# Loading k and q of the first batch whole, in place of by column ranges, in a linear-attention and MLP kernel

## The chip, the cores and the metric

The kernel runs on one core of a Trainium2 chip. The metric is device time in microseconds (us) of one execution; the median over several runs is compared. Engines: PE is the matmul array (PEld its weight loads), DVE the vector engine, ACT the activation engine, POOL the GpSimd engine, SP the engine that only issues transfers. Transfers issued from SP and from POOL run on the same 16 DMA engines, in two queues (q1 for SP, q0 for POOL).

## The reference

Inputs are q, k, v of shape (8, 8, 576, 64) (batch, heads, sequence, head size) and two MLP weights, 512x2048 and 2048x512. The attention is linear, with a cosine weighting of positions; its result, put back into rows of 512, goes through the MLP.

```
def phi(x, c, s):                       # c, s: cos and sin of pi/2 * position / S
    r = np.maximum(x, 0.0)
    return np.concatenate([r * c, r * s], axis=-1)
kv  = einsum('bhsf,bhsd->bhfd', phi(k), v)
z   = sum over s of phi(k)
num = einsum('bhsf,bhfd->bhsd', phi(q), kv)
den = einsum('bhsf,bhf->bhs', phi(q), z)[..., None] + 1e-06
x   = (num / den) as rows of 4608 x 512
h   = x @ w_in
out = (h * sigmoid(1.702 * h)) @ w_out
```

## The kernel before, in words

The eight batches go one after the other. For each, phi(k) and phi(q) are made on DVE and ACT, PE forms the 128x64 state of every head (kv), divides on DVE, transposes the result and runs the MLP; batch b+1's attention is woven into batch b's MLP. The order on every engine is written out by hand: instructions of an engine run in the order in which the program has them, with waits by semaphore.

The change touches the head of the program, the work on batch 0 ahead of its MLP. Names and lines there:

- L65 to L67: four loads from SP, k into kf and q into qf, 128 partitions by 4 head pairs by 576 floats. Each is cut by columns: k at 192, q at 256 floats. A column range of 64 floats is one position index j (0 to 8) of the nine that each partition holds, so k's first load has j = 0, 1, 2 and q's first j = 0 to 3. A partition's 576 floats of one head pair are contiguous in HBM, 2304 bytes.
- L153 and L154: a copy of one float of kf on POOL, in column 0. It keeps what follows it on POOL waiting until the load that holds that column has landed. Behind it POOL issues v of batch 0 in two loads (L156, into a part of the tile named sums, with a cast to bf16) and w_in's first two parts (L138).
- L161 trig: relu(k) times cos or sin for one j: two operations for each j, on DVE (L169), ACT (L167) or POOL. L819 to L827 give kr for j = 0, 1, 3, 4, 5 and the cos of 6 to DVE, j = 2, the sin of 6, and 7, 8 to ACT. L837 to L841 and L847 do the same for q into qn: j = 0, 1 on DVE, 2 to 5 and 7 on ACT, 6 and 8 on POOL.
- L778 idle: matmuls on zeros, 128x512, whose result nobody reads. L819 puts nine ahead of all else on PE. L831 puts two more between the k-sums.
- L247 ksum_mm: a matmul of kr for one j with a selector of 2 columns: the sum over k, over all nine j; L254 ksum_rows copies it out on DVE (L256), L258 ksum_turn turns it with small matmuls (L260) and a copy (L262).
- L197 qturn_pe: transposes of qn on PE (L205); L208 qevac copies them out on DVE (L215) or ACT (L213).
- L232 kv_mm: the products of kr and v, in two halves of four heads (L237), copied out by DVE (L245). L271 num_half, L286 div_half, L295 x_half: numerators (L276), division (L289, L291), transposes (L299) and a copy on ACT (L301). Then the first MLP matmuls (L882, L365).
- On POOL, behind the w_in loads: qn of j = 6, a copy of one element of v (L842, it waits for v's second load), the rest of w_in, k of batch 1, and parts of w_out.

Of the kernel before, what the change touches and what calls it, by code (L numbers as in the profile page):

```python
# [20 lines left out]
def kernel(  # L21
# [9 lines left out]
    nc = tc.nc  # L31
    B, H, S, D = q.shape
# [24 lines left out]
    def src_of(src, b, i0=0, i1=NI):  # L57
        return src[b, 2 * i0:2 * i1].rearrange("(i hh) (p j) d -> (hh p) i (j d)", hh=2, j=NS)

    qf = one.tile([128, 2560], F32, name="qf")  # L60
    kf, vf = [one.tile([128, NI, S], F32, name=n) for n in ("kf", "vf")]
    sums = one.tile([128, 4, d_ff], BF16, name="sums")
    vb = sums.rearrange("p n e -> p (n e)")[:, 0:NI * S].rearrange("p (i e) -> p i e", i=NI)
    qf0 = qf[:, 0:NI * S].rearrange("p (i e) -> p i e", i=NI)
    for t, src, cut in ((kf, k, 192), (qf0, q, 256)):  # L65
        nc.sync.dma_start(out=t[:, :, 0:cut], in_=src_of(src, 0)[:, :, 0:cut])
        nc.sync.dma_start(out=t[:, :, cut:S], in_=src_of(src, 0)[:, :, cut:S])  # L67


    NP = NS + 5  # L70
# [707 lines left out]
    def idle(n, cols=512):  # L778
        w = pmm.tile([128, 512], F32, name="mm")
        for _ in range(n):  # L780
            nc.tensor.matmul(w[:, 0:cols], warm[:, 0:128], warm[:, 0:cols], start=True, stop=True)
# [34 lines left out]
        xturn_evac(b, 4)  # L816


    idle(9)  # L819
    for j in (0, 1):  # L820
        trig(kr, kf, j)
    trig(kr, kf, 2, act=True)
# [321 lines left out]
```

## Time and profile before

| what | us |
|---|---|
| median of 3 runs (275.0 to 275.77) | 275.01 |
| the profiled execution's own time | 275.49 |
| its span in the profile | 273.4 |
| PE busy (97% of the span) | 265.7 |
| DVE busy (76%) | 207.8 |
| ACT busy (64%) | 174.8 |
| POOL busy (15%) | 42.4 |
| head, 0 to 15.3: PE busy / DVE busy / ACT busy | 12.70 / 10.29 / 12.15 |

Durations come from that one profiled execution, on a time scale that starts with its span. Busy time says how long an engine worked, not whether the end waited for it; for that the views of waits and of the chain that ended last are read. A duration in the timeline holds the pipeline's latency too, so consecutive operations overlap: what one costs its engine is the distance from its start to the next one's start. DMA rows give the time from the start of the issue to the landing that the waiting engine sees, and packets and bytes can be counted for any window of the span.

### The profile page before, as it was taken

To read this page: it belongs to the slowest core of one execution; us is meant where nothing else is said; L and a number is where in the kernel's file an instruction comes from. 1 tells how busy PE (TensorE), PEld (TensorE's weight loads), DVE (VectorE), ACT (ScalarE), POOL (GpSimd) and SP (SyncE) were. 2 spreads that over 40 slices of the span, in tenths; PEclk is the share of its full clock that TensorE was granted. 3 is DMA by queue.
4 is the path that set the end of the run, shared out by engine and by line. 5 is a ranking of instruction groups with operands and counts; after the bars stand their busy time and mean duration, and the time that the engine had idled before them with its cause. 6 is when DMAs were issued, how large, how long until landed. Compare 5 with 4: busy or idle time off the path is not lost.

```text
span 273.4 us, 7042 instructions
## 1 busy us (share of the span) xinstructions
PE 265.7 (97%) x2847; PEld 207.2 (76%) x2868; DVE 207.8 (76%) x487; ACT 174.8 (64%) x317; POOL 42.4 (15%) x71
## 2 busy tenths in 40 slices
PE   7899999999999999999999999999999999999994
PEld 2585645856987799778877887788778976999983
DVE  3956866698879798879887988888888994745741
ACT  5957642585199728983888387848783147677621
POOL 5691000000121012101110012001200173000410
PEclk9999999999999999999999999999999999999999
DMA  7999999999999996999898789796970654000333
GB/s 233 254 211 298 274 296 143 273 304 175 332 185 284 240 267 192 227 236 256 243 250 236 210 175 285 162 304 127 293 159 2 108 153 137 0 2 0 88 107 115
DMA packets 73663, 53.60 MB, mean 196 GB/s; under 512 B 52736, under 2 KB 63488, under 8 KB 73632
## 3 DMA queue, kind: packets, MB, share of 16 engines
q1 hardware_dynamic: 67504, 36.97, 58.3%
q0 software_dynamic: 6128, 16.19, 23.9%
q8 instruction: 22, 0.36, 0.6%
q14 instruction: 9, 0.07, 0.1%
HBM read 36.70 MB, written 9.44 MB: 169 GB/s over the span
## 4 chain that ended last, share of the span: by engine, by line
PE 93%; DMA 4%; DVE 1%; issue 1%; ACT 0%; POOL 0%
PE mm L520 31%; PE mm L658 16%; PE mm L365 13%; PE at L721 9%; PE mm L421 5%; PE at L520 4%; PE mm L396 4%; PE at L237 4%; PE at L310 3%; DMA sums<-in_v_dram 2%; DMA kf<-in_k_dram 1%; PE at L342 1%; PE mm L389 1%; DVE xn L325 1%; PE mm L205 0%
## 5 line engine op out<-in xcount | busy, mean ns | idle before, releaser
L520 PEld LDWEIGHTS <-sums 128*128 128x128 bf16 x448 | 42.5, 98 | 4.8
L526 POOL DMA_DIRECT2D out_dram<-ysb x24 | 17.4, 727 | 180.2 <-DVE inv L323 88.2
L520 PE MATMUL mm<-wsum,sums 128*128 128x256 bf16 x336 | 39.9, 272 | 0.0
L365 PE MATMUL mm<-xT,w_in 128*128 128x512 bf16 (+1 forms) x239 | 38.7, 305 | 0.5
L520 PEld LDWEIGHTS <-g 128*128 128x128 bf16 x336 | 32.0, 98 | 3.6
L371 ACT ACTIVATE g<-mm 128x512 bf16<-128x512 f32 x42 | 24.1, 598 | 10.9 <-PE mm L365 10.9
L365 PEld LDWEIGHTS <-w_in 128*128 128x128 bf16 x248 | 21.3, 114 | 11.5
L721 PE MATMUL at<-xT,w_in 128*128 128x512 bf16 x110 | 27.8, 379 | 0.5
L325 DVE TENSOR_TENSOR xn<-at,inv 128x512 bf16<-128x512 f32 x39 | 27.0, 691 | 1.3
L169 DVE TENSOR_SCALAR kr<-kf,cosw 128x256 bf16<-128x256 f32 x69 | 24.6, 357 | 3.0 <-DMA kf<-in_k_dram 3.0
L520 PE MATMUL mm<-w_out_sb,g 128*128 128x256 bf16 x224 | 26.6, 273 | 0.0
L169 DVE TENSOR_SCALAR kr<-kf,sinw 128x256 bf16<-128x256 f32 x68 | 23.6, 347 | 0.0
L658 PE MATMUL mm<-xT,w_in 128*128 128x256 bf16 x152 | 22.0, 273 | 0.0
L658 PE MATMUL mm<-xT,gt 128*128 128x256 bf16 x160 | 21.5, 272 | 0.0
L658 PEld LDWEIGHTS <-w_in 128*128 128x128 bf16 x168 | 18.6, 114 | 3.3
L183 ACT ACTIVATE qn<-qf,cosw 128x512 bf16<-128x512 f32 (+1 forms) x27 | 19.2, 711 | 1.5 <-DMA qf<-in_q_dram 1.1
L658 PEld LDWEIGHTS <-gt 128*128 128x128 bf16 x160 | 17.6, 113 | 3.0 <-issue 1.2
L721 PEld LDWEIGHTS <-w_in 128*128 128x128 bf16 x120 | 13.5, 113 | 8.2
L183 ACT ACTIVATE qn<-qf,sinw 128x512 bf16<-128x512 f32 (+1 forms) x27 | 19.2, 709 | 0.0
L371 ACT ACTIVATE g<-at 128x512 bf16<-128x512 f32 x30 | 17.5, 598 | 2.0 <-PE at L721 1.3
L535 ACT ACTIVATE kept_p<-mm 128x512 f32<-128x512 f32 (+1 forms) x15 | 8.5, 566 | 16.0 <-PE mm L520 16.0
L535 ACT ACTIVATE kept_u<-mm 128x512 f32<-128x512 f32 (+1 forms) x8 | 4.4, 544 | 20.6 <-PE mm L520 20.6
(175 smaller groups left out, 471.3 us busy)
## 6 DMA issues: line engine op xcount, KB each, us to landing
kf<-in_k_dram SPq DMA_DIRECT2D x6, 1152.0 KB, 9.2
vf<-in_v_dram SPq DMA_DIRECT2D x6, 1152.0 KB, 6.5
qf<-in_q_dram SPq DMA_DIRECT2D x6, 1024.0 KB, 6.3
out_dram<-ysb POOLq DMA_DIRECT2D x24, 256.0 KB, 5.1
w_out_sb<-in_moe_w_out_dram POOLq DMA_DIRECT2D x4, 512.0 KB, 17.7
kf<-in_k_dram POOLq DMA_DIRECT2D x1, 1152.0 KB, 13.4
vf<-in_v_dram POOLq DMA_DIRECT2D x1, 1152.0 KB, 20.8
w_in<-in_moe_w_in_dram POOLq DMA_DIRECT2D x2, 512.0 KB, 10.0
```

Of the source, the lines that this page charges most:

```text
L169: eng.tensor_scalar(o, i, 0.0, w[:, j:j + 1], op0=MAX, op1=MUL)
L183: nc.scalar.activation(o, i, AF.Relu, scale=sc)
L237: nc.tensor.matmul(st["kv", i][:, hh, ds(col, n)], kr[r, j, i, :], rhs(r, i, j), start=(j == 0), stop=(j == NS - 1))
L325: nc.vector.tensor_tensor(xn, pv[:, :, :, 0:64], inv.unsqueeze(3).to_broadcast([128, 2, 4, 64]), op=MUL)
L365: nc.tensor.matmul(hp[fc][:, t0:t1], wcol(kc, fc), x[b][:, kc, t0:t1], start=(kc == 0), stop=(kc == KC - 1))
L371: nc.scalar.activation(gT[fc // 4][:, fc % 4], hp.pop(fc), AF.Gelu_apprx_sigmoid)
L421: nc.tensor.matmul(yp[b, t, c0][:, c0:c1], w, w_out_sb[:, fc, c0:c1], start=(fc == 0), stop=(fc == FC - 1))
L520: nc.tensor.matmul(bank[to][c], lhs, rhs, start=opens, stop=(fc == HF - 1), skip_group_check=True)
L526: eng.dma_start(out=dst[:, 2 * i + c0:2 * i + c1, ts(n, HD)], in_=t[:, c0:c1])
L535: nc.scalar.activation(o, i, AF.Identity)
L658: nc.tensor.matmul(to[:, j], lhs, rhs, start=(opens and j == 0 and k == 0), stop=(k == 1), skip_group_check=True)
L721: nc.tensor.matmul(hp[fc], wcol(kc, fc), x[b][:, kc], start=(kc == 0), stop=(kc == KC - 1))
```

## The change

k and q of batch 0 are each loaded by one transfer of 128x4x576 floats, in pieces of 2304 bytes, where there were two. The order on SP is k, then q, as before. Every operation that waited for one of a tensor's two loads now waits for its only one. The nine idle matmuls at the start of PE's work become eleven. Nothing else changes in the order of any engine.

```
-    for t, src, cut in ((kf, k, 192), (qf0, q, 256)):
-        nc.sync.dma_start(out=t[:, :, 0:cut], in_=src_of(src, 0)[:, :, 0:cut])
-        nc.sync.dma_start(out=t[:, :, cut:S], in_=src_of(src, 0)[:, :, cut:S])
+    for t, src in ((kf, k), (qf0, q)):
+        nc.sync.dma_start(out=t, in_=src_of(src, 0))
...
-    idle(9)
+    idle(11)
```

## The prediction

> **What bounds the kernel now.** I read the page's busy shares first (PE 97% of the span), then who waited for whom on PE, because an edit to two loads can only cost what PE ends up waiting for. That view of the whole span has three rows:
>
> ```profile
> PE mm L781 <- DVE wsum L81: 1.2, 1, 1.2
> PE mm L251 <- DVE kr L169: 0.8, 2, 0.6
> PE mm L299 <- DVE xh L291: 0.2, 1, 0.2
> ```
>
> All three lie before 15.3 us: from there to the end PE waits for nobody for more than a few tenths in all. So the kernel is a head of some 15 us, paced by loads, DVE, ACT and small matmuls, and then a PE stream. A delay of the head moves the end by the same amount; a gain likewise. The change touches only the head.
>
> The chain that ended last, in order of time, names this in the head:
>
> ```profile
> 0.79 3.90 DMA kf<-in_k_dram
> 4.75 0.12 POOL gate L154
> 4.87 6.49 DMA sums<-in_v_dram
> ...
> 11.41 0.70 PE at L237 x36
> ```
>
> k's first column range lands, POOL's copy at L154 passes, v is issued, v lands, the k-v products start. But the timeline of DVE shows a second chain that is just as tight:
>
> ```profile
> 4.80 0.35 DVE L169 TENSOR_SCALAR kr<-kf,cosw 128x256 bf16<-128x256 f32 x1 [2.01 <-DMA kf<-in_k_dram]
> ...
> 5.33 0.56 DVE L169 TENSOR_SCALAR kr<-kf,cosw 128x256 bf16<-128x256 f32 x1
> 5.81 0.33 DVE L169 TENSOR_SCALAR kr<-kf,sinw 128x256 bf16<-128x256 f32 x1
> 6.84 0.59 DVE L169 TENSOR_SCALAR kr<-kf,cosw 128x256 bf16<-128x256 f32 x1 [0.70 <-DMA kf<-in_k_dram]
> ...
> 8.88 0.34 DVE L169 TENSOR_SCALAR kr<-kf,cosw 128x256 bf16<-128x256 f32 x1
> 9.14 0.34 DVE L169 TENSOR_SCALAR qn<-qf,cosw 128x256 bf16<-128x256 f32 x1
> ...
> 10.19 0.67 DVE L256 CAST wsum<-mm 2x512 bf16<-2x512 f32 x1
> 10.79 1.27 DVE L215 COPY qT<-mm 128x1024 bf16<-128x1024 bf16 x2
> 11.99 0.17 DVE L262 CAST kvs<-mm 128x8 bf16<-128x8 f32 x1
> 12.15 0.43 DVE L245 CAST kvs<-at 128x256 bf16<-128x256 f32 x1
> ```
>
> (Columns: start, duration, instruction, idle time before it.) DVE does 4 kr operations on the first column range, idles 0.70 us, and then has no gap from 6.84 to 12.58, up to the evacuation of the first k-v product. That product ended at 12.11 (11.41 and 0.70), and DVE was free for it at 12.15: v's chain and DVE's meet within 0.04 us.
>
> **The loads.** The rows of DMA issues (KB, us from issue to landing), each from a window of the trace: the two parts of k, and one later load of v, of the form that k's load now takes (576 contiguous floats, 512 pieces):
>
> ```profile
> kf<-in_k_dram SPq DMA_DIRECT2D x1, 384.0 KB, 3.9
> kf<-in_k_dram SPq DMA_DIRECT2D x1, 768.0 KB, 5.5
> vf<-in_v_dram SPq DMA_DIRECT2D x1, 1152.0 KB, 6.0
> ```
>
> Issued at 0.79 and 1.31, the parts land at 4.69 and about 6.8. Counted in quarter microseconds, the first packets move in the one from 1.75; by 3.0 some 165 KB have moved (1 KB = 1000 bytes in my byte counts), and then the rate is 332 GB/s with 768-byte packets and 399 with 1536-byte ones. k's 1180 KB are through at about 5.67; the landing comes 1.1 us later.
>
> What one transfer does to this, from two sides. First, by its bytes: the same 165 KB up to 3.0, then (1180-165)/396 = 2.56 us at the 396 GB/s that 2304-byte packets show in the later loads, gives 5.56, and with 1.1 us a landing at 6.66. Second, by whole loads of that shape: 6.0 us is the shortest of six for v (the others up to 12.1, beside other traffic), so 6.79; that issue took 0.58 us against 0.45 for k's first, so perhaps 6.66. Do larger packets ramp faster? The later v loads show full rate only 1.2 to 1.3 us after their first packet, with 136 to 205 KB moved by then: no. I take 6.7 for the landing, and 6.80 for the first kr operation (4.69 to 4.80 now). Lower bound: full rate from the first packet, worked out below as a rival; upper: 6.9.
>
> **The sum.** Removed: the early start of 4 DVE and 2 ACT operations at 4.8.
> - DVE: the 7 kr operations that now start at 6.84 come behind the 4 that lost their place. Those took 4.80 to 6.14 = 1.34 us. New start 6.80+1.34 = 8.14, against 6.84: **+1.30 us**, and all of DVE's unbroken work behind it moves with it: the kr for the last k-sum at L251, the qn for L205, the copies at L256, L215, L262 and L245.
> - The durations inside: 3 of the 11 kr operations are 0.56 to 0.59 instead of 0.35, each while POOL was issuing its four loads (4.87 to 8.06). The four issues now fall inside DVE's kr work as well. I count the same 3; none or four would give -0.7 or +0.2.
> - ACT: 7 kr operations at 0.40 from 6.78 end at 9.6 against 8.86 (+0.75). That is less than DVE's, so it hides behind DVE: the ACT evacuation at 12.85 then waits for transposes that are over a microsecond late themselves.
> - POOL: the copy at L154 now waits for the whole of k, 2.0 us longer. Behind it queue both v loads, both w_in loads, and qn of j=6. v is issued at about 6.9 instead of 4.87. That costs nothing as long as v's packets could not have moved earlier. They did not: between 4.87 and 8.5 no packet of POOL's queue moves, and the first one comes as q's last go through. Beside the later SP loads it is the same (the store issued at 134.85 has no packet until 137.25, when v's load is through); with less ahead of it, the one issued at 100.72 moves in the quarter from 101.95, some 1.3 us behind its issue. 6.9+1.3 = 8.2. With larger packets q's last go through at 3.0+(2359-165)/396 = 8.54, about 0.45 before the present 9.0. So v lands at about 11.0 to 11.4, and the products that need it are due only at 11.41+1.30 = 12.7: v's chain is covered by 1.3 us. If that cover is gone, v is the rival below. The w_in loads queue behind v in the same stream and come no later than now.
> - q: all of it lands around 9.6 and its first reader, ACT, asks at 9.6, DVE at 10.4: covered on DVE; on ACT a few tenths late would still be under DVE's 1.30.
> - The two more idle matmuls: 0.43 us each while the array is slow; the nine end at 5.26, eleven by 6.12. The first k-sum comes 0.66 us behind the first kr, at 7.46. Hidden by 1.3 us; nothing.
> - The two issues that go (0.48 and 0.51 us on SP): SP is idle from 2.9 on; nothing.
>
> So +1.30 us on 275.49 (the profiled execution; span 273.4) = 276.8. That execution is 0.48 above the median of the runs, 275.01; carried over, **276.3 us**. With landings from 6.4 to 6.9 and DVE's long operations from none to four, +0.3 to +1.7; the likeliest part is +0.9 to +1.5.
>
> **Rivals.**
> - *k lands early.* If one transfer reached the fastest quarter of the later v loads, 433 GB/s, from its first packet at 1.8, it would be through at 1.8+1180/433 = 4.53 and land at 5.6: kr starts at 5.7, +0.2 us, 275.2. For it: fewer, longer packets. Against: no load in this trace ramps at once. The Trainium skill's page "DMA: Bandwidth & Descriptors" ("Anatomy of one DMA — SWDGE (gpsimd) path") fits, for POOL's queue, 2.0 us and the bytes at 436 GB/s; an estimate by that page is 4.7 us for k, landing at 5.5, total 275.1. The trace disagrees for SP's loads: 6.0 us at the least.
> - *v becomes the bound.* If v's first packet comes a fixed 3.7 us behind its issue (issued at 4.87, first packet in the quarter from 8.5, as now), the issue 2.0 us later moves v's landing from 11.37 to 13.4, past DVE's 12.7: +2.0 us, 277.0. For it: just this one pair of numbers. Against: the 1.3 us above.
> - *Not slower: only v's chain counts.* The chain view names v, not DVE. If DVE's work had slack where the timeline shows none, the end would follow v, which could start 0.45 us earlier once q is through sooner: 274.6. It decides only if the head can absorb 1.3 us on DVE; against it stands the 5.7 us on DVE without a gap.
> - *The array slows down.* Between 6.1 and 7.46 PE is idle (now 0.20, 0.60). The nine idle matmuls start 0.43 us apart, the two at L831 (6.54, 6.77) 0.23. If the longer gap cost that speed, PE's 3.8 us of work between 10 and 14 (its busy time in the half-microsecond windows) would take up to twice as long; some of it lies in waits. Taking a third, +1.2 on top: 277.5. The granted clock in the rows is 1.00 throughout and decides nothing here. The Trainium skill, "TensorE: Matmul & The Clock Gate", Part 1, wants an idle window of about 3.4 us before the clock drops; by that rule 1.3 us changes nothing. The trace of before has no such gap to show it.
>
> **How the numbers follow.** Forecast 0.60 (0.54 slower, 0.05 same, 0.01 faster, by how early k lands); k early 0.12 (0.10 same, 0.02 faster); v the bound 0.13; v's chain alone 0.08 (0.05 same, 0.03 faster); slow array 0.07. "Same" is within 0.3%, 0.83 us, about what a measurement of this kernel can tell. Slower 0.74, same 0.20, faster 0.06. The range goes from just under the early k (275.2) to just short of the slow array (277.5).
>
> **What would show it.** In the changed kernel: one k row of 1152 KB with 5.8 to 6.1 us to landing; first kr on DVE at 6.7 to 6.9; last kr operation starting at 10.2 instead of 8.88; v landing before 11.5; the first products at L237 near 12.7 and released by DVE or PE, not by v; PE without new waits behind 17 us. A k landing before 6.0, a v landing after 12.7, or matmuls at L237 and L205 of longer spacing would make the prediction wrong in that order.

## The result, and the profile after

The changed kernel takes **277.31 us** (median of 6 runs, 277.08 to 277.99) against 275.08 (median of 6, 275.0 to 275.97): a ratio of the means of 1.0075, 95% interval 1.0056 to 1.0093. The profiled execution took 277.11 us with a span of 275.1, against 275.49 and 273.4. So the traces explain +1.62 us; of the +2.23 between the medians the other 0.61 comes from where the two profiled executions lie: before's 0.41 above its median, after's 0.20 below its own. In the changed kernel most line numbers are one less than before (L169 is now L168, L237 is L236).

The view of waits on PE, whole span, kernel after (waited for: us in total, times, longest):

```profile
PE mm L250 <- DVE kr L168: 1.4, 2, 0.9
...
PE mm L204 <- DVE qn L168: 0.8, 2, 0.5
PE mm L657 <- DVE gt L666: 0.3, 1, 0.3
```

PE waits longer for DVE's kr (1.4 against 0.8) and newly for DVE's qn; the third row is new too, and lies at 91 us, far behind the head. The chain that ended last, kernel after, its part in the head (start, duration, what):

```profile
0.79 5.39 DMA kf<-in_k_dram
...
6.28 4.19 DVE kr L168 x11
10.47 1.58 DVE qn L168 x4
...
12.10 0.84 PE mm L204 x12
12.94 0.18 PE mm L259 x4
13.12 0.63 PE at L236 x36
```

v is no longer in it. k lands as a whole, then eleven kr and four qn operations on DVE follow without a gap, then the transposes and the first k-v products, at 13.05 by the timeline instead of 11.41: +1.64. DVE's first xn, the last step of the head, starts at 16.83 instead of 15.17: +1.66, which is the +1.62 of the whole execution. (Later on 0.3 more comes in at L657, and the end gives about as much back: the last store takes 2.8 us from ACT's last operation to the end of the span, against 3.1.)

Now DVE and POOL in the timeline of the kernel after (start, duration, instruction, idle time before it):

```profile
6.28 0.35 DVE L168 TENSOR_SCALAR kr<-kf,cosw 128x256 bf16<-128x256 f32 x1 [3.49 <-DMA kf<-in_k_dram]
6.36 1.68 POOL L155 DMA_DIRECT2D sums<-in_v_dram  x2
...
6.81 0.56 DVE L168 TENSOR_SCALAR kr<-kf,cosw 128x256 bf16<-128x256 f32 x1
...
7.55 0.60 DVE L168 TENSOR_SCALAR kr<-kf,cosw 128x256 bf16<-128x256 f32 x1
...
8.01 1.53 POOL L137 DMA_DIRECT2D w_in<-in_moe_w_in_dram  x2
...
8.33 0.58 DVE L168 TENSOR_SCALAR kr<-kf,cosw 128x256 bf16<-128x256 f32 x1
...
9.09 0.56 DVE L168 TENSOR_SCALAR kr<-kf,cosw 128x256 bf16<-128x256 f32 x1
...
9.55 1.20 POOL L168 TENSOR_SCALAR qn<-qf,cosw 128x256 bf16<-128x256 f32 x1
9.58 0.63 DVE L168 TENSOR_SCALAR kr<-kf,sinw 128x256 bf16<-128x256 f32 x1
10.13 0.34 DVE L168 TENSOR_SCALAR kr<-kf,cosw 128x256 bf16<-128x256 f32 x1
10.39 0.50 DVE L168 TENSOR_SCALAR qn<-qf,cosw 128x256 bf16<-128x256 f32 x1
...
10.72 1.17 POOL L168 TENSOR_SCALAR qn<-qf,sinw 128x256 bf16<-128x256 f32 x1
10.82 0.56 DVE L168 TENSOR_SCALAR qn<-qf,sinw 128x256 bf16<-128x256 f32 x1
...
11.56 0.48 DVE L168 TENSOR_SCALAR qn<-qf,sinw 128x256 bf16<-128x256 f32 x1
11.96 0.67 DVE L255 CAST wsum<-mm 2x512 bf16<-2x512 f32 x1
```

The operations between these rows take 0.33 to 0.35. Two things differ from the forecast. The first kr starts at 6.28, not 6.80. And eight of the fifteen operations are long (0.48 to 0.63), not three: one for each of POOL's four load issues (L155, L137; 6.36 to 9.54), and four of the six beside POOL's own qn of j = 6 (9.55 to 11.89). In the kernel before, that POOL work began at 10.32, when DVE's qn had ended and DVE was copying out of PSUM (the memory that PE writes its results to); the copies kept their 0.67 and 1.27 beside it. The row of before:

```profile
10.32 1.14 POOL L169 TENSOR_SCALAR qn<-qf,cosw 128x256 bf16<-128x256 f32 x1 [2.26 <-ACT qn L167]
```

DVE reaches the copy at L255/L256 at 11.96 instead of 10.19, +1.77. By starts in the two timelines: first kr 6.28 against 6.84, -0.56; the four operations that lost their early place, 6.28 to 7.55, +1.27; the other seven kr 2.84 against 2.30, +0.54; the four qn 1.57 against 1.05, +0.52.

### The profile page after: what moved, and what is told of

It is laid out like the page before. It is cut to its first block, busy times and chain, and to the rows that moved or that the text cites. A ratio compares the mean times of both kernels' runs of the same rounds, so it can differ in the third digit from the quotient of the medians.

```text
span 275.1 us, 7063 instructions
## 1 busy us (share of the span) xinstructions
PE 267.5 (97%) x2870; PEld 207.3 (75%) x2870; DVE 208.6 (76%) x487; ACT 175.2 (64%) x317; POOL 42.4 (15%) x71
## 4 chain that ended last, share of the span: by engine, by line
PE 92%; DVE 4%; DMA 2%; ACT 0%; issue 0%; DVEq 0%
PE mm L519 31%; PE mm L657 15%; PE mm L364 13%; PE at L720 9%; PE mm L420 5%; PE at L519 4%; PE mm L395 4%; PE at L236 3%; PE at L309 3%; DMA kf<-in_k_dram 2%; DVE kr L168 2%; PE at L341 1%; PE mm L204 1%; PE mm L388 1%; DVE qn L168 1%; DVE xn L324 1%
## 5 line engine op out<-in xcount | busy, mean ns | idle before, releaser
L364 PE MATMUL mm<-xT,w_in 128*128 128x512 bf16 (+1 forms) x248 | 39.3, 307 | 0.0
L720 PE MATMUL at<-xT,w_in 128*128 128x512 bf16 x120 | 29.2, 379 | 0.0
L168 DVE TENSOR_SCALAR kr<-kf,cosw 128x256 bf16<-128x256 f32 x69 | 24.7, 358 | 3.5 <-DMA kf<-in_k_dram 3.5
L168 DVE TENSOR_SCALAR kr<-kf,sinw 128x256 bf16<-128x256 f32 x68 | 23.8, 350 | 0.0
L657 PE MATMUL mm<-xT,w_in 128*128 128x256 bf16 x152 | 22.0, 273 | 0.0
L657 PE MATMUL mm<-xT,gt 128*128 128x256 bf16 x160 | 21.5, 272 | 0.3 <-DVE gt L666 0.3
L657 PEld LDWEIGHTS <-w_in 128*128 128x128 bf16 x168 | 18.6, 113 | 3.3
L657 PEld LDWEIGHTS <-gt 128*128 128x128 bf16 x160 | 17.6, 113 | 3.3 <-issue 1.6
L309 PEld LDWEIGHTS <-qT 128*128 128x128 bf16 x312 | 14.0, 97 | 3.0 <-issue 1.8
```

The lines of the kernel that those rows point to most:

```text
L168: eng.tensor_scalar(o, i, 0.0, w[:, j:j + 1], op0=MAX, op1=MUL)
L309: nc.tensor.matmul(ps[:, h // 4, ds((h % 4) * 65, 65)], qT[:, h, ts(c, 128)], kvs_of(h), start=not eps_too, stop=(not eps_too or h % 4 == ...
L364: nc.tensor.matmul(hp[fc][:, t0:t1], wcol(kc, fc), x[b][:, kc, t0:t1], start=(kc == 0), stop=(kc == KC - 1))
L657: nc.tensor.matmul(to[:, j], lhs, rhs, start=(opens and j == 0 and k == 0), stop=(k == 1), skip_group_check=True)
L720: nc.tensor.matmul(hp[fc], wcol(kc, fc), x[b][:, kc], start=(kc == 0), stop=(kc == KC - 1))
```

## The experiments

**Theory**: the head is as late as DVE's block of fifteen operations behind k's only landing; POOL's issues and POOL's qn stretch it; q's load and the idle matmuls cost nothing. **Rivals**: q's load has a part in it; v's later start bounds; the array is slower behind a longer idle gap. Each kernel is the one named, with one edit.

### Only k whole, and only q whole

From the kernel after:

```
-    for t, src in ((kf, k), (qf0, q)):
-        nc.sync.dma_start(out=t, in_=src_of(src, 0))
+    nc.sync.dma_start(out=kf, in_=src_of(k, 0))
+    nc.sync.dma_start(out=qf0[:, :, 0:256], in_=src_of(q, 0)[:, :, 0:256])
+    nc.sync.dma_start(out=qf0[:, :, 256:S], in_=src_of(q, 0)[:, :, 256:S])
```

> The changed kernel with q loaded in two column ranges again; k stays whole. Theory (the loss is DVE's kr work starting as one block behind k's only landing, and POOL's work falling beside it): k lands near 6.2, kr on DVE starts near 6.3, and the head is as late as in the changed kernel within 0.3 us: 276.9 to 277.4 in all. Rival (the loss comes from q landing whole, because ACT and DVE ask for its first part early): back to 275.0 to 275.5.

Measured: 277.19 us, ratio to before 1.0072 (1.006 to 1.0084); profiled 277.09. k lands at 6.28, DVE starts at 6.38, seven operations are long, the products start at 12.93, xn at 16.71. The chain runs through DVE as in the kernel after:

```profile
6.38 4.11 DVE kr L169 x11
```

k's load alone gives nearly the whole loss: 1.54 of the 1.66 in the head.

The opposite half keeps k's two loads and nine idle matmuls:

```
+    nc.sync.dma_start(out=kf[:, :, 0:192], in_=src_of(k, 0)[:, :, 0:192])
+    nc.sync.dma_start(out=kf[:, :, 192:S], in_=src_of(k, 0)[:, :, 192:S])
+    nc.sync.dma_start(out=qf0, in_=src_of(q, 0))
...
-    idle(11)
+    idle(9)
```

> The kernel before with only q loaded whole. Theory: k's parts land at 4.7 and 6.8 as before, so DVE's kr work stays at 4.80 and 6.84; q lands near 9.2, which delays ACT's first qn from 8.86 to about 9.25 and may let POOL's qn of j=6 start beside DVE's qn (some 0.1 to 0.5 us more on DVE): 275.1 to 275.7 in all. Rival (q whole is the loss): 276.8 or more.

Measured: 276.61 us, 1.0053 (1.004 to 1.0067); profiled 276.42. The theory missed: q whole by itself is slower too. Two rows of this kernel show how, one of its chain and one of its timeline:

```profile
1.84 7.60 DMA qf<-in_q_dram
```

```profile
9.46 0.35 DVE L169 TENSOR_SCALAR qn<-qf,cosw 128x256 bf16<-128x256 f32 x1 [0.66 <-DMA qf<-in_q_dram]
```

With k still early, DVE is through with kr at 8.80, 0.66 us before q has landed; with q in two pieces its first columns were there by then. POOL's qn waits for q as well, starts at 9.63 in place of 10.32, and two of DVE's four qn beside it are long (0.57, 0.49), which adds 0.39. Both parts are partly hidden, since k's parts landed 0.4 earlier in this execution than in the first profile of before. xn starts at 15.77, +0.60. The two losses don't add (0.60 and 1.54 in the head, 1.66 together): with k whole, DVE reaches its qn only at 10.39, and q's landing is covered. So "q costs nothing" holds only under k's loss. Of this kernel's +0.93 in the profiled execution 0.33 lies behind the head and is not explained, except for a wait of 0.2 at L658.

### POOL's part in DVE's long operations

The kernel after with qn of j = 6 on ACT:

```
-    for j in (2, 3, 4, 5, 7):
+    for j in (2, 3, 4, 5, 6, 7):
...
-    trig(qn0, qf0, 6, eng=nc.gpsimd)
```

> The changed kernel with qn of j=6 made on ACT instead of POOL. Theory (POOL's two operations at 9.55 to 11.9 stretch DVE's kr and qn operations beside them): the DVE operations from 9.5 on take 0.34 each again, the four long ones beside POOL's load issues stay; DVE's qn ends 0.5 to 0.8 us earlier; ACT's two more operations fit in its wait before 14.34; 276.4 to 276.8 in all. Rival (the stretched operations come from v's transfers, which then run): they stay long, and the time is 277.1 to 277.6.

Measured: 276.69 us, 1.0048 (1.0036 to 1.006), 0.6 under the kernel after by medians. Rows of its timeline and of its chain:

```profile
10.40 0.34 DVE L168 TENSOR_SCALAR qn<-qf,cosw 128x256 bf16<-128x256 f32 x1
10.66 0.34 DVE L168 TENSOR_SCALAR qn<-qf,sinw 128x256 bf16<-128x256 f32 x1
...
11.93 0.68 DVE L255 CAST wsum<-mm 2x512 bf16<-2x512 f32 x1 [0.40 <-PE mm L250]
```

```profile
9.32 2.57 PE mm L250 x6
```

The four long operations beside the load issues remain (7.11 to 9.39); the four beside POOL's qn are back at 0.33 to 0.34. That part of the stretch is shown. The profiled execution, at 277.09 the slowest of the six, doesn't show the gain, because PE took its place: six k-sums in 2.57 us, behind a pair of idle matmuls (L830) that together take 1.03 us instead of 0.61. Here the record names the reason, a halved TensorE clock. The row of one window (busy time of PE, PEld, DVE, ACT and POOL with their instructions, granted clock, DMA share, GB/s) reads 0.50 where the kernel after has 1.00:

```profile
10.00:11.00 1.00, 1.00 (x4) 0.34 (x3) 1.00 (x5) 1.00 (x3) 0.00 (x0) 0.50 1.12 176
```

In windows of a quarter microsecond the clock is 0.50 from about 8.3 to 11.7.

The kernel after without POOL's copy in front of the load issues:

```
-    nc.gpsimd.tensor_copy(gate[0:1, 0:1], kf[0:1, 0, 0:1])
```

> The changed kernel without the copy on POOL that waits for k, so that POOL issues v and w_in from about 2.3 us. Theory (a load issue on POOL stretches one DVE operation beside it by 0.22 us; POOL's queue moves no packets while SP's has work): the four issues fall before 6.2, where DVE is idle; k lands near 6.2 still; DVE's chain is 0.7 to 0.9 us shorter; 276.3 to 276.7 in all. Rival (the two queues share the DMA engines): v's packets run beside k's and q's, k lands 1 us later or more, 278 or more.

Measured: 277.8 us, 1.0089 (1.0076 to 1.0102); profiled 277.94. Two rows of the timeline, then the two queues between 7.5 and 8.0 us (packets, MB, share of 16 engines):

```profile
7.50 0.35 DVE L167 TENSOR_SCALAR kr<-kf,cosw 128x256 bf16<-128x256 f32 x1
...
11.36 0.35 DVE L167 TENSOR_SCALAR qn<-qf,cosw 128x256 bf16<-128x256 f32 x1 [1.95 <-DMA qf<-in_q_dram]
```

```profile
q0 software_dynamic: 42, 0.05, 55.6%
q1 hardware_dynamic: 40, 0.09, 53.0%
```

The four issues now run from 2.24 to 5.4, ahead of DVE's work, and all eleven kr operations take 0.35: the other part of the stretch is shown, and it is the issuing that does it, since the same loads' packets move beside these operations. The expected gain in time did not come; the price is elsewhere. The first packet of v moves between 6.25 and 6.5, when k's are through, and from 7.0 to 10.0 v and q each take about half of the engines' packet time. q lands at 11.34, and DVE waits 1.95 us for it.

### The idle matmuls, and the two kernels once more

The kernel after with `idle(9)` for `idle(11)`:

> The changed kernel with nine idle matmuls. Theory (the two more are hidden in PE's wait for k): 277.1 to 277.5, the same within 0.1%, unless the longer idle gap (5.2 to 6.95) makes the array slow again, which would show as 0.43 us between the two matmuls at L831 and cost up to 0.6 us more. Rival (the two cost their own time): 0.4 to 0.9 us less.

Measured: 277.61 us, 1.0079 (1.0067 to 1.0091); profiled 277.33. The idle gap ahead of the first k-sum grows to 1.82 us, the pair at L830 is 0.43 apart, the k-sums are slow until 11.4, and the head still follows DVE (xn 16.97, first kr 6.42: 0.14 later each). The two added matmuls neither gain nor cost anything that these runs can tell.

Kernel before again, no edit:

> The kernel before, profiled a second time, because its first profiled execution (275.49) was 0.4 above its median. Theory (the landing of k's parts differs from execution to execution by some tenths, and the head moves with it): k's parts land near 4.3 and 6.4 instead of 4.7 and 6.8, every later start of the head is about 0.4 earlier than in the first profile, and this execution takes 275.0 to 275.2. Rival (the loads land as in the first profile, and the difference comes from elsewhere): 4.7 and 6.8 again.

Measured: 275.8 us, one run. The first kr operations on k's two parts start at 4.71 and 6.76 (4.80 and 6.84 in the first profile) and the head is 0.07 earlier, yet the time is 0.31 longer. The theory that the landing explains before's spread falls; by the starts on PE the difference arises in two steps, 0.2 between 83 and 85 us and 0.14 between 158 and 162 us, without a wait that the profile lists.

Kernel after again, no edit:

> The changed kernel, profiled a second time. Theory: k lands at 6.2 to 6.5 as in the runs with k whole so far, again with eight long operations among DVE's 15 kr and qn ones, four beside POOL's load issues and four beside its qn of j=6; 277.0 to 277.5. Rival (the number of long operations was chance): three to five long ones and about 0.7 us less.

Measured: 277.58 us, one run. The first kr starts at 6.31, and the same eight operations are long, at 6.84, 7.58, 8.36, 9.12, 9.60, 10.42, 10.84 and 11.58. Landing and stretch are no accident of one execution.

### Another cut for k

The kernel before with k cut at 256:

```
-    for t, src, cut in ((kf, k, 192), (qf0, q, 256)):
+    for t, src, cut in ((kf, k, 256), (qf0, q, 256)):
```

> The kernel before with k cut at 256 floats instead of 192, so that k's first part has j = 0 to 3. Theory (DVE's kr work is the bound and idles 0.7 us for k's second part): the first part lands about 0.25 us later, DVE does 6 operations on it instead of 4 and does not wait for the second part; DVE's kr ends 0.3 to 0.5 us earlier; v's landing then ends last, so 274.7 to 275.1 in all. Rival (the gate on k's first part, and with it v, decides): 0.2 to 0.3 us slower than before.

Measured: 275.55 us (12 runs), 1.0009 (1.0 to 1.0017). The expected gain did not come. The first part landed at 5.33, 0.64 later than at a cut of 192 and not 0.25 later. DVE no longer waits for k's second part, but four operations are long in place of three, and its first qn starts at 9.24 against 9.14 before: the later start uses up what the wait had cost. The chain of this kernel goes on through PE:

```profile
8.50 2.30 PE mm L251 x6
10.80 1.00 PE mm L205 x16
```

In this execution the array was slow too (L831's pair 1.03 us instead of 0.60), and DVE waits 0.46 us for the last k-sum at L256: most of the +0.55 of this head is the array's. No version tried beats the kernel before.

### Head and total

| kernel | xn starts, against before | profiled time, against before |
|---|---|---|
| after | +1.66 | +1.62 |
| only k whole | +1.54 | +1.60 |
| only q whole | +0.60 | +0.93 |
| qn of j = 6 on ACT | +1.64 | +1.60 |
| without POOL's copy | +2.50 | +2.45 |
| nine idle matmuls | +1.80 | +1.84 |
| k cut at 256 | +0.55 | +0.65 |
| before again | -0.07 | +0.31 |
| after again | +1.68 | +2.09 |

In six of the nine the head gives the total within 0.1 us; three hold 0.33 to 0.41 from behind it.

## Why the prediction was right in sign and short in size

- *What bounds.* Right. The end follows the head (within 0.1 us in six of the nine profiles), and in the kernel after the head follows DVE, not v, which the chain view of before had named. Reading the second, equally tight chain out of the timeline was what mattered.
- *k's landing, forecast 6.66 to 6.79, 6.18 measured.* Too late by half a microsecond. The bytes were right: counted in the trace, k's last are through at about 5.53, against 5.56 forecast. Wrong was the term of 1.1 us from there to the landing; it is 0.65. The row, forecast at 5.8 to 6.1:

```profile
kf<-in_k_dram SPq DMA_DIRECT2D x1, 1152.0 KB, 5.4
```

  The sixteen packets under 512 bytes that come at the end of a load, as many as there are DMA engines, tell more: all in the half microsecond from 5.25 in the kernel after; in the kernel before those of k's second part lie between 5.25 and 6.5, and the load lands behind the last of them. The forecast's tail came from a load whose engines, read so, finished up to a microsecond apart. Why one large load keeps them together was not tested.
- *Four operations lose their place.* Right: +1.27 against 1.34.
- *"I count the same 3; none or four would give -0.7 or +0.2".* The step that failed most: there are eight, and the five more than counted cost 1.06. Three of the four load issues already fell on kr operations in before, and all four do now, one long operation for each; behind them comes POOL's qn, which the forecast did not look at as a neighbour of DVE at all. It starts at 9.55 instead of 10.32, and DVE's qn start at 10.39 instead of 9.14, so the two meet. With q in two pieces and k whole they meet as well (POOL's qn from 9.77, three long operations beside it). The load issues and the qn are each shown (the two kernels on POOL's part). The Trainium skill's page "SBUF — State Buffer" ("SBUF: two separate sides") says that GpSimd and VectorE share a pair of ports, held by one instruction at a time while the other fully blocks, and means on VectorE's side operations in a two-port mode or with two inputs in SBUF, the on-chip memory that the loads fill. No run here tells which mode these operations ran in. The runs agree that the two engines disturb each other, and only on operations that read SBUF; but a POOL operation of 1.20 us lengthened two of the three DVE operations beside it by 0.13 to 0.28 us each and didn't stop any for its length, so here the measured row decides.
- *The sum.* Forecast +1.30 in the head, +1.66 measured: -0.5 of landing and +1.06 of stretch against the forecast, which partly cancelled. At the median the forecast of 276.3 lies 1.0 under 277.31. Of that, 0.32 is this sum (1.62 against 1.30 in the profiled executions). The rest is the step "carried over": the profiled execution of before lay 0.48 above the median it was set against, that of after 0.20 below its own. Such tenths arise behind the head, as the table shows, and did not carry over here.
- *Luck.* Both sizes left the spreads that the sum gave them: the landing was to be 6.4 to 6.9 and the long operations none to four. The last kr operation starts at 10.13, as forecast (10.2), only because the two errors cancel there. The sum's own +0.3 to +1.7 on the median ends at 276.7, below the 277.31 measured; the stated range reaches 277.5 only for the sake of rivals, a late v and a slow array, that the profile of the kernel after does not show.
- *v is covered.* Right. v's first half, issued at 6.36, lands at 10.46 (11.36 before), 2.6 us ahead of its products at 13.05, where 1.3 were forecast. Its second half, for which the forecast had no term, lands at 13.6, 0.9 ahead of its products at 14.49. But "v's packets could not have moved earlier" was too strong: without POOL's copy they move beside q's, once k's are through.
- *q is covered.* Right in this kernel; wrong as a property of the edit, as q alone shows.
- *Idle matmuls, SP's issues: nothing.* Right. The slow array did not show in the kernel after (L830's pair 0.61), but in four of the other eight profiles the pair takes 1.03 us. In one of these, qn on ACT, the granted clock reads 0.50 from about 8.3 to 11.7; in the other three it reads 1.00 all through the head. The idle gaps there are 0.83, 0.99, 1.69 and 1.82 us; profiles with 0.93, 0.95 and 1.32 stayed fast. So a gap of that size can go with a slow array, and length alone doesn't decide it. The Trainium skill's page "TensorE: Matmul & The Clock Gate" (Part 1) wants about 3.4 us of idle and says that the window runs freely; these gaps are all shorter than that, while a cause that depends on phase would fit the scatter. The half clock of the one profile lasts about as long as that window, 3.4 us. That the phase decides is not shown.
- *"PE without new waits behind 17 us".* Wrong by one: 0.2 to 0.3 us at L657 to L658 for DVE's gt, in the profiles of after (both), only q whole, nine idle matmuls, qn on ACT and the kernel without the copy, not in those of before (both), only k whole and the other cut. So all six profiles with q whole have it and none of the four with q in two parts. What links q's load to a wait at 91 us stays open; no run was made for it.

## What to carry to other kernels

The cut of a load is worth what the first consumer does on the early piece, here four DVE operations, 1.27 us, and the transfer as one piece gave back only 0.56 of it. When a gate moves a batch of GpSimd work, lay that work beside VectorE's new timeline operation by operation: a VectorE operation out of SBUF that meets a load issue or a GpSimd operation took 0.13 to 0.28 us longer here, and that counts if VectorE is in the chain. And test both halves of a double edit, since one loss can hide the other.

## What the runs showed of the hardware

- A DVE operation 128x256, fp32 to bf16 out of SBUF, takes 0.33 to 0.35 us; beside a load issue on POOL 0.56 to 0.60, one operation for each of the issues it meets (the kernels before and after); beside a POOL operation of the same form two of three take 0.48 to 0.63. Copies out of PSUM (0.67, 1.27) were not stretched.
- A load of 1152 KB from SP, the first in its queue, landed 5.4 to 5.7 us from its issue (5.39, 5.49, 5.53, 5.69 in four profiles), 0.65 us behind its last data in the first of them.
- Without POOL's copy, the queue that POOL feeds moved nothing while k's load ran, though v was issued at 2.24, and then took as much of the engines' packet time as q's load (55.6% and 53.0%), for 0.05 against 0.09 MB.
- Behind an idle gap of 1.69 us on PE the granted clock read 0.50 for some 3.4 us in one profile (qn on ACT). In three others matmuls 128x512 ran just as slowly behind gaps of 0.83 to 1.82 us while the clock read 1.00, so their distance, 0.43 us instead of 0.2, is the surer sign.
